# Alternating the half and the queue of the Toeplitz strip loads, and one eviction for two channels, in a long-convolution kernel

## The chip, the cores and the metric

The kernel runs on one core of a Trainium2 chip. The metric is the device time in microseconds (us) of the whole program. Executions of one kernel agree within about 0.3%, so effects below one per cent were timed in several rounds against the kernel before on the same chip. The record marks each timed run as fast or slow by its time and its granted clock. The stage lengths below are each read from one profiled execution; the experiment e4, which loads its strips as the kernel before does, has a stage 3 us longer, so differences of that size mean nothing.

## The reference, cut to what matters

```python
def _attn_ref(x, h):                  # x: (8, 5696, 128), h: (5696, 128), float32
    L = 2 * S                         # a causal convolution along the sequence, per channel d
    y = irfft(rfft(x, n=L, axis=1) * rfft(h, n=L, axis=0)[None], n=L, axis=1)[:, :S, :]
    return y
def _moe_ref(x, w_theta, w_tok_r, w_tok_i, w_ch):     # fed with the y of above
    theta = x @ w_theta
    y = einsum('ts,bsd->btd', w_tok_r, x*cos(theta)) + einsum('ts,bsd->btd', w_tok_i, x*sin(theta))
    u = x + y
    return u + maximum(u @ w_ch, 0)
```

The change touches only the first half, the convolution. The kernel computes it per channel `d` as a block-Toeplitz matrix product on the matmul engine.

## The kernel before: the parts that matter

Each channel needs 45 blocks of 128 x 128 weights. They are cut from "strips": partition `p` of a strip holds the padded filter `h_pad[d]` from position `j0 + p` on, so each partition holds the one above it shifted by one element. A strip serves 15 matmuls. Only 64 partitions are loaded from memory; the other 64 are the same data 64 columns later, and VectorE (DVE) copies them.

```python
    KS = 15                                                # blocks per strip, 3 strips per channel
    ...
    with tc.tile_pool(name="conv_sbuf", bufs=6) as csb, \
         tc.tile_pool(name="conv_psum", bufs=2, space=PSUM) as cps:
        for d in range(D):                                 # 128 channels
            psum = cps.tile([P, NT * B], F32, tag="convps")          # 128 x 360
            for k0 in range(0, NT, KS):
                k1 = k0 + KS; w = KS * P; j0 = P * k0
                strip = csb.tile([P, KS * P + 64], BF16, tag="strip")
                own, other, c0, c1 = (lower half, upper half, 0, 64) if d % 2 == 0 else \
                                     (upper half, lower half, 64, 0)
                nc.sync.dma_start(strip[own, :w + 64], bass.AP(...h_pad, d * HW + j0,     # L151
                                          ap=[[1, 64], [1, w + 64]]))   # 64 rows, 1 element apart
                nc.vector.tensor_copy(strip[other, c0:c0 + w], strip[own, c1:c1 + w])     # L154
                for k in range(k0, k1):
                    ntj = NT - k; c = c0 + (k - k0) * P
                    nc.tensor.matmul(psum[:, B * k: B * k + B * ntj], strip[:, c:c + P],  # L158
                                     x_sb2[:, d, :B * ntj],
                                     start=(k == 0), stop=(k == NT - 1))
            nc.scalar.activation(                                                         # L162
                y_sb[:, :, :, d].rearrange("q t b -> q (t b)"), psum, AF.Copy)
```

(The slices are spelled in words.) The moving operand shrinks from 360 columns at the first block to 8 at the last, so the first strip of a channel keeps the matmul engine much longer than the third. `y_sb` has the channel as its innermost dimension: the eviction of one channel (the copy of its finished sums out of `psum`) writes 360 single bf16 values per partition, 256 bytes apart.

## Time and profile before

| | before |
|---|---|
| time, median of its first 3 runs | 2369.0 us |
| convolution, first to last L158 matmul | 108.2 to 598.0 us, 490 us |
| the same without stalls (128 channels of 3.63 us) | 465 us |
| strip: bytes, median time from issue to landing | 254 KB, 4.6 us |
| one eviction (ScalarE, ACT) | 1.777 us |

The groups of the page (line, engine, operation, output<-input, shapes, count; busy us and mean ns of one; idle time of the engine just before them and what ended it) show the three lines that matter. PE is the matmul engine, DVE is VectorE, ACT is ScalarE:

```profile
L158 PE MATMUL psum<-x_sb,strip 128*128 128x360 bf16 (+44 forms) x5760 | 474.1, 243 | 17.0 <-DVE strip L154 15.2
...
L154 DVE COPY strip<-strip 64x1920 bf16<-64x1920 bf16 x384 | 250.7, 655 | 239.3 <-DMA strip<-h_pad 205.1
...
L162 ACT ACTIVATE y_sb<-psum 128x360 bf16<-128x360 f32 x128 | 227.4, 1777 | 264.4 <-PE psum L158 264.4
```

The eviction costs 1.777 us for 360 elements per partition. DVE waits 205 us for strip DMAs, but what counts is how much of that reaches PE. The view of the matmuls' line (duration min/median/max, first and last start) and the view by stretches (busy us and instruction count per engine, then granted clock, DMA share, GB/s) give the stage:

```profile
L158 PE MATMUL psum<-x_sb,strip x5760: 166/243/501, 108.2 to 598.0; 128*128 128x360 bf16 x5, 128*128 128x128 bf16 x5, 128*128 128x256 bf16 x5, 128*128 128x24 bf16 x5
```

```profile
core 0: us, PE busy (x) PEld busy (x) DVE busy (x) ACT busy (x) POOL busy (x), PEclk, DMA share, GB/s
108.00:598.00 490.00, 473.93 (x5760) 406.32 (x5759) 249.38 (x382) 225.78 (x128) 0.00 (x0) 0.99 0.75 199
```

PE is busy 474 of 490 us at a granted clock of 0.99 (the share of full speed that PE was given), so it bounds the stage. The timeline gives the pace that PE has when nothing disturbs it: four evictions in a row, each released by the last matmul of its channel, start 3.63 us apart (columns: start, duration, engine, line, operation, count, idle before and releaser):

```profile
117.96 1.78 ACT L162 ACTIVATE y_sb<-psum 128x360 bf16<-128x360 f32 x1 [1.73 <-PE psum L158]
...
121.59 1.78 ACT L162 ACTIVATE y_sb<-psum 128x360 bf16<-128x360 f32 x1 [1.85 <-PE psum L158]
...
125.22 1.77 ACT L162 ACTIVATE y_sb<-psum 128x360 bf16<-128x360 f32 x1 [1.85 <-PE psum L158]
...
128.84 1.78 ACT L162 ACTIVATE y_sb<-psum 128x360 bf16<-128x360 f32 x1 [1.86 <-PE psum L158]
```

128 channels at that pace are 465 us, so about 25 us of the stage are lost. The list of waits names what PE waits for (total us, times, longest):

```profile
engine line waited for: us in total, times, longest us
PE psum L158 <- DVE strip L154: 15.2, 33, 0.9
```

It is the copied strip, and behind the copy the strip's DMA. The timeline shows one such place: the copy starts only at 162.24 us, after 1.65 us of waiting for its DMA, and the next channel's first matmul follows 0.06 us after the copy's end:

```profile
162.24 0.65 DVE L154 COPY strip<-strip 64x1920 bf16<-64x1920 bf16 x1 [1.65 <-DMA strip<-h_pad]
...
162.95 1.30 PE L158 MATMUL psum<-x_sb,strip 128*128 128x360 bf16 x8 [0.55 <-DVE strip L154]
```

One strip of 254 KB per 1.21 us (a third of 3.63) is 210 GB/s; the stage moves 199 GB/s. The page's list of DMA issues (size, median us from issue to landing; its KB are 1024 bytes, so 248.0 KB are the 254 KB of the text):

```profile
strip<-h_pad SPq DMA_DIRECT2D x384, 248.0 KB, 4.6
```

### The profile page before, as it was taken

The page shows a single profiled execution, that of the slowest core. Times are in us where ns is not written, and L with a number is a line of the kernel's source. Part 1 is how long each engine was busy: PE and PEld are TensorE (multiplying, and loading weights), DVE is VectorE, ACT ScalarE, POOL GpSimd, SP SyncE. Part 2 cuts the span into 40 slices and gives each one's busy share as a digit, 9 for nine tenths or more (in the row PEclk, how much of TensorE's full clock was granted, in tenths as well). Part 3 has the DMA queues.
Part 4 walks back from the last instruction along what each step waited for, and adds up shares of the span by engine and source line. Part 5 has one row for each costly group of instructions (what it writes and reads, how often), then busy time and mean ns, then how long its engine had stood idle before and what let it go on. Part 6 is the DMA issues. An engine that isn't in the chain of part 4 may idle for free.

```text
span 2367.9 us, 39718 instructions
## 1 busy us (share of the span) xinstructions
PE 2191.0 (93%) x14513; PEld 1216.4 (51%) x14686; DVE 1649.6 (70%) x2997; ACT 639.2 (27%) x733; POOL 796.1 (34%) x1474
## 2 busy tenths in 40 slices
PE   4699999999666999999999999799999999999997
PEld 1188888888432444444444444234444444444443
DVE  5655555555577888887787776687677677677774
ACT  3544444444862333332232000001111111111111
POOL 0000000000201544544446564344544544544540
PEclk7599999999978999999999999899999999999998
DMA  9977777777998988988789997967877977977872
GB/s 238 251 204 203 200 204 202 202 197 202 232 284 218 164 156 168 164 165 156 134 168 164 159 151 128 286 101 134 156 136 130 160 134 134 160 132 136 151 135 54
DMA packets 435332, 405.51 MB, mean 171 GB/s; under 512 B 66497, under 2 KB 370625, under 8 KB 435009
## 3 DMA queue, kind: packets, MB, share of 16 engines
q0 software_dynamic: 222816, 131.33, 42.4%
q1 hardware_dynamic: 209296, 260.55, 38.9%
q10 hardware_dynamic: 3024, 11.08, 1.3%
q8 instruction: 116, 1.90, 0.3%
q14 instruction: 80, 0.65, 0.1%
HBM read 449.27 MB, written 84.75 MB: 226 GB/s over the span
## 4 chain that ended last, share of the span: by engine, by line
PE 70%; DMA 15%; DVE 8%; issue 3%; POOL 2%; ACT 1%; SPq 1%; DVEq 0%; ACTq 0%; POOLq 0%
PE m L598 51%; PE psum L158 14%; DMA strip<-h_pad 6%; DMA tmp<-in_x_dram 2%; DVE c L605 2%; POOL wb L326 2%; DMA wb<-in_moe_w_tok_r_dram 2%; DMA wb<-in_moe_w_tok_i_dram 2%; DMA h_bf<-in_h_dram 1%; DVE wt L335 1%; DVE strip L154 1%; PE v L419 1%; PE utp L412 1%; PE m L560 1%; PE m L562 1%
## 5 line engine op out<-in xcount | busy, mean ns | idle before, releaser
L326 POOL DMA_DIRECT2D wb<-in_moe_w_tok_i_dram x720 | 388.7, 547 | 801.7 <-DVE wt L335 713.8
L326 POOL DMA_DIRECT2D wb<-in_moe_w_tok_r_dram x720 | 387.6, 546 | 714.4 <-PE psum L158 594.3
L158 PE MATMUL psum<-x_sb,strip 128*128 128x360 bf16 (+44 forms) x5760 | 474.1, 243 | 17.0 <-DVE strip L154 15.2
L598 PE MATMUL m<-b,wt 128*128 128x512 bf16 x1892 | 453.7, 383 | 26.9 <-DVE wt L335 9.8
L158 PEld LDWEIGHTS <-strip 128*128 128x128 bf16 x5760 | 406.5, 98 | 85.4 <-DVE strip L154 21.2
L335 DVE STREAM_TRANSPOSE wt<-wb 128x384 f32<-128x384 f32 (+2 forms) x720 | 359.8, 524 | 123.1 <-PE m L598 73.5
L154 DVE COPY strip<-strip 64x1920 bf16<-64x1920 bf16 x384 | 250.7, 655 | 239.3 <-DMA strip<-h_pad 205.1
L598 PEld LDWEIGHTS <-wt 128*128 128x128 bf16 x1936 | 190.6, 99 | 259.8 <-issue 27.6
L162 ACT ACTIVATE y_sb<-psum 128x360 bf16<-128x360 f32 x128 | 227.4, 1777 | 264.4 <-PE psum L158 264.4
L605 DVE TENSOR_TENSOR c<-c,m 128x512 f32<-128x512 f32 x440 | 284.0, 671 | 0.0
L414 ACT ACTIVATE uts<-utp 128x512 bf16<-128x512 bf16 (+1 forms) x90 | 53.3, 592 | 616.7 <-PE utp L412 616.7
L409 ACT ACTIVATE ub<-c 128x512 bf16<-128x512 f32 (+1 forms) x90 | 56.5, 628 | 226.6 <-DVE c L605 226.3
L121 PE MATMUL rps<-tmpbf,R_bf 128*128 128x512 bf16 x88 | 45.7, 620 | 52.1 <-DVE tmpbf L118 52.0
L185 ACT ACTIVATE yT<-tpz 128x512 bf16<-128x512 bf16 x68 | 39.7, 596 | 191.5 <-PE tpz L181 191.5
L118 DVE CAST tmpbf<-tmp 128x1024 bf16<-128x1024 f32 x45 | 56.7, 1267 | 33.3 <-DMA tmp<-in_x_dram 33.1
L199 ACT ACTIVATE red<-theta_ps,magic 128x512 f32<-128x512 f32 x46 | 31.6, 687 | 151.3 <-PE theta_ps L197 116.9
L421 DVE SCALAR_TENSOR_TENSOR c<-v,c 128x512 f32<-128x512 f32 (+1 forms) x90 | 61.6, 684 | 11.3 <-PE v L419 10.8
L123 ACT ACTIVATE x_sb<-rps 128x1024 bf16<-128x1024 f32 x45 | 46.1, 1024 | 57.8 <-PE rps L121 50.1
L219 ACT ACTIVATE mag<-mag,half_pi 128x512 f32<-128x512 f32 (+1 forms) x68 | 57.8, 850 | 0.2
L605 DVE TENSOR_TENSOR c<-yy,m 128x512 f32<-128x512 bf16 x88 | 56.1, 679 | 0.9 <-PE m L598 0.9
L121 PEld LDWEIGHTS <-R_bf 128*128 128x128 bf16 x90 | 6.2, 111 | 89.5 <-DVE tmpbf L118 80.8
L217 ACT ACTIVATE mag<-red 128x512 f32<-128x512 f32 x46 | 29.0, 630 | 77.6 <-DVE red L201 77.6
(2759 smaller groups left out, 2967.7 us busy)
## 6 DMA issues: line engine op xcount, KB each, us to landing
strip<-h_pad SPq DMA_DIRECT2D x384, 248.0 KB, 4.6
wb<-in_moe_w_tok_r_dram POOLq DMA_DIRECT2D x352, 96.0 KB, 4.4
wb<-in_moe_w_tok_i_dram POOLq DMA_DIRECT2D x352, 96.0 KB, 4.6
wb<-in_moe_w_tok_r_dram POOLq DMA_DIRECT2D x352, 80.0 KB, 4.3
wb<-in_moe_w_tok_i_dram POOLq DMA_DIRECT2D x352, 80.0 KB, 3.7
tmp<-in_x_dram SPq DMA_DIRECT2D x44, 512.0 KB, 5.8
cp_hbm<-c SPq DMA_DIRECT2D x88, 256.0 KB, 2.5
c<-cp_hbm SPq DMA_DIRECT2D x88, 256.0 KB, 4.6
```

Of the source, the lines that this page charges most:

```text
L118: nc.vector.tensor_copy(tmpbf, tmp.transpose([0, 2, 1]))
L154: nc.vector.tensor_copy(strip[other, c0:c0 + w], strip[own, c1:c1 + w])
L158: nc.tensor.matmul(psum[:, B * k: B * k + B * ntj], strip[:, c:c + P], x_sb2[:, d, :B * ntj], start=(k == 0), stop=(k == NT - 1))
L162: nc.scalar.activation(y_sb[:, :, :, d].rearrange("q t b -> q (t b)"), psum, AF.Copy)
L219: nc.scalar.activation(mag, mag, AF.Sin, bias=half_pi, scale=-TWO_PI)
L326: nc.gpsimd.dma_start(wb[32 * i:32 * i + 32, :ng, :nj * 64], bass.AP(tensor=a.tensor, offset=a.offset + row0 * S + p * H + i * QR + j0 * 6 ...
L335: nc.vector.transpose(wt.rearrange("p j t r -> p (j t r)").bitcast(F32).rearrange("p (j g t) -> p g j t", j=TJ, g=4)[:, :ng, :nj], wb[:, : ...
L409: nc.scalar.activation(ub[:m].rearrange("p b d -> p (b d)"), c[:m], AF.Copy)
L414: nc.scalar.activation(uts[:, :, :m], utp[:, :, :m], AF.Copy)
L421: nc.vector.scalar_tensor_tensor(c[:m], v[:m], 0.0, c[:m], op0=ALU.max, op1=ALU.add)
L598: nc.tensor.matmul(ms[q], a[q][:, j, :, r], bts[jj][q][:, r, :], start=(jj == 0 and r == 0), stop=(jj == NJ - 1 and r == 1 and q not in left))
L605: nc.vector.tensor_tensor(c, z, ms[q], op=op)
```

## The change

The intent: let two strips in flight go to different halves of the partitions, so that the DMA engines can write both halves at once, and let two queues feed them; and halve the work of ACT by evicting two channels in one instruction, which then writes two neighbouring bf16 values (4 bytes) at each place.

```diff
         for d in range(D):
-            psum = cps.tile([P, NT * B], F32, tag="convps")
+            if d % 2 == 0:
+                pair = cps.tile([P, 2, 512], F32, tag="convps")
+            psum = pair[:, d % 2, :NT * B]
             for k0 in range(0, NT, KS):
 ...
-                own, other, c0, c1 = ((slice(0, 64), slice(64, P), 0, 64) if d % 2 == 0 else
+                n_ = d * 3 + k0 // KS
+                own, other, c0, c1 = ((slice(0, 64), slice(64, P), 0, 64) if n_ % 2 == 0 else
                                       (slice(64, P), slice(0, 64), 64, 0))
-                nc.sync.dma_start(strip[own, :w + 64],
+                eng = nc.sync if n_ % 2 == 0 else nc.scalar
+                eng.dma_start(strip[own, :w + 64],
 ...
-            nc.scalar.activation(
-                y_sb[:, :, :, d].rearrange("q t b -> q (t b)"), psum, AF.Copy)
+            if d % 2 == 1:
+                nc.scalar.activation(
+                    y_sb[:, :, :, d - 1:d + 1].rearrange("q t b e -> q (t b) e"),
+                    pair[:, :, :NT * B].rearrange("q e n -> q n e"), AF.Copy)
```

More of the change, by code (lines that the diff above doesn't have):

```diff
@@ L147 @@
                 strip = csb.tile([P, KS * P + 64], BF16, tag="strip")
-                own, other, c0, c1 = ((slice(0, 64), slice(64, P), 0, 64) if d % 2 == 0 else
+                n_ = d * 3 + k0 // KS
+                own, other, c0, c1 = ((slice(0, 64), slice(64, P), 0, 64) if n_ % 2 == 0 else
                                       (slice(64, P), slice(0, 64), 64, 0))
-                nc.sync.dma_start(strip[own, :w + 64],
-                                  bass.AP(tensor=h_pad.tensor, offset=h_pad.offset + d * HW + j0,
-                                          ap=[[1, 64], [1, w + 64]]))
+                eng = nc.sync if n_ % 2 == 0 else nc.scalar
+                eng.dma_start(strip[own, :w + 64],
+                              bass.AP(tensor=h_pad.tensor, offset=h_pad.offset + d * HW + j0,
+                                      ap=[[1, 64], [1, w + 64]]))
                 nc.vector.tensor_copy(strip[other, c0:c0 + w], strip[own, c1:c1 + w])
```

## The prediction

> **What bounds the kernel now.** The change touches only the convolution stage, from the first L158 matmul at 108.2 us to the last at 598.0 us (the view of line L158): 490 us of 2368. There the view by stretches gives PE 57.5 to 58.4 us busy in each 60 us at a granted clock of 1.00, ACT about 28. PE bounds the stage. In the timeline, undisturbed channels follow each other every 3.63 us (L162 starts at 117.96, 121.59, 125.22, 128.84), so 128 channels would take 465 us. Some 25 us of the stage are stalls; that is all the change can win, 1.1%.
>
> The stalls come from strips that arrive late: the list of waits has PE behind the L154 copy 33 times (15.2 us) and its weight loads 40 times (20.6 us); that copy waited 205 us for strip DMAs. A strip is 64 partitions x 3968 B = 254 KB. One every 1.21 us (the PE pace) is 210 GB/s; the stage runs at 200 to 204, with a median of 4.6 us from issue to landing, 3.3 us at best. The Trainium skill ("SBUF — State Buffer", "Door 1: The DMA port swizzle") says 64 partitions reach 8 of 16 ports, about 218 GB/s. The trace agrees: the transfers sit just under that. Three strips in a row use one half.
>
> **What changes.** Bytes, copies (655 ns) and matmuls stay. Halves alternate on every strip and two queues feed them, so two strips in flight can use different ports. The same page ("Can I just issue two DMAs to hit both halves?") measured only +6% for this. Even +6% on 200 GB/s is 212, just above what PE needs; I expect somewhat more, and landing about 3.5 to 4 us.
>
> ACT gets 192 issues (0.44 us each on SP now, about 85 us) and 64 double evictions for 128 of 1.777 us. One eviction of 360 elements into 2-byte pieces 256 B apart costs 4.4 ns an element, while L123 with 16-byte pieces costs 1.0; the cost is in the scattered write. Pairs have the same number of pieces, so my estimate is 1.8 to 2.1 us for a pair, saving about 100 us of ACT, all off the critical path.
>
> **The risk.** ACT works in order. The strip that reuses the buffer of a pair's last strip becomes issuable as the pair's eviction does, and probably queues behind it. Its loop is eviction + landing + copy 0.65 + its matmuls 0.6 + about 0.15: with 1.9 and 3.6 us that is 6.9 us, inside the 7.26 us that PE needs for a pair. If the pair's eviction took 3.4 us (every element paying the scattered price), the loop would be 8.3 us or more and add 65 us or more over 64 pairs.
>
> The end of the stage gains a double eviction and four PSUM banks instead of two held until then: under 1 us. Later stages should shift unchanged.
>
> **Predicted.** Most of the 25 us of stall goes, 5 to 7 us remain: 2350 us, 8 in 10 between 2338 and 2385. Faster by over 2% (under 2322) would need more than the stage's stalls: 0.03. Within 2%: 0.86. Slower: 0.11.
>
> **What would show it.** Right: first to last L158 matmul in about 470 us; PE's wait for L154 from 15 us to under 5; stage rate near 210 GB/s; median landing under 4.2 us; L162 x64 at about 1.9 us. Wrong: landing still 4.6 us and the same stalls (halves do not overlap: about 2369); or regular PE waits once per pair for a strip issued by ACT right after L162 (queue order); or L162 above 3 us.
>
> **What would make it wrong.** A slow pair eviction; late issues in ACT's in-order queue; engines that serialise the halves; a lower granted clock when PE has no gaps.

## The result, and the profile after

The median went from 2367.65 us (4 runs) to 2355.34 us (4 runs, 2354.32 to 2358.01). The ratio is 0.9943, with a 95% interval of 0.9928 to 0.9958: faster, though by less than 2%. Here and below a ratio is the mean time of one kernel's fast runs over that of the other's fast runs of the same rounds, so it is not quite the ratio of the medians. The kernel is 13.5 us faster (0.0057 of 2368), inside the predicted range of 2338 to 2385, but 5 us short of the predicted 2350.

The groups after, with the line numbers of the new kernel (L158 is now the copy, L162 the matmul, L167 the eviction):

```profile
L162 PE MATMUL pair<-x_sb,strip 128*128 128x360 bf16 (+44 forms) x5760 | 472.0, 243 | 8.9 <-DVE strip L158 7.0
...
L158 DVE COPY strip<-strip 64x1920 bf16<-64x1920 bf16 x384 | 251.5, 655 | 228.1 <-DMA strip<-h_pad 194.8
...
L167 ACT ACTIVATE y_sb<-pair 128x720 bf16<-128x720 f32 x64 | 50.9, 795 | 429.8 <-PE pair L162 368.1
```

The stage by the line of its matmuls and by stretches:

```profile
L162 PE MATMUL pair<-x_sb,strip x5760: 166/243/497, 108.1 to 587.7; 128*128 128x360 bf16 x5, 128*128 128x128 bf16 x5, 128*128 128x256 bf16 x5, 128*128 128x24 bf16 x5
```

```profile
core 0: us, PE busy (x) PEld busy (x) DVE busy (x) ACT busy (x) POOL busy (x), PEclk, DMA share, GB/s
108.00:588.00 480.00, 472.00 (x5760) 403.93 (x5759) 250.80 (x383) 50.25 (x65) 0.00 (x0) 1.00 0.72 203
```

PE's waits, and the DMA issues:

```profile
PE pair L162 <- DVE strip L158: 7.0, 18, 1.3
```

```profile
strip<-h_pad SPq DMA_DIRECT2D x192, 248.0 KB, 4.3
strip<-h_pad ACTq DMA_DIRECT2D x192, 248.0 KB, 4.3
```

The convolution went from 490 to 480 us. PE's wait for the copied strip halved, from 15.2 to 7.0 us, but did not go away. The landing time fell only from 4.6 to 4.3 us. The eviction, now of twice the data, takes 0.795 us, less than half of what one channel took before. So four questions are open. Which of the three parts made the gain? Why are about 15 us of stalls left (480 against 465)? Why is the pair eviction so cheap? And did the in-order ACT queue, the risk of the prediction, cost anything?

### The profile page after: what moved, and what is told of

Same layout as the page of the kernel before. It is cut to its first block, busy times and chain, and to the rows that moved or that the text cites. A ratio compares the mean times of both kernels' runs of the same rounds, so it can differ in the third digit from the quotient of the medians.

```text
span 2352.5 us, 39824 instructions
## 1 busy us (share of the span) xinstructions
PE 2191.6 (93%) x14686; PEld 1210.8 (51%) x14686; DVE 1650.1 (70%) x2997; ACT 462.6 (20%) x669; POOL 798.2 (34%) x1474
## 4 chain that ended last, share of the span: by engine, by line
PE 77%; DMA 13%; DVE 6%; issue 2%; ACT 1%; SPq 1%; POOL 1%; DVEq 0%; ACTq 0%; POOLq 0%
PE m L604 56%; PE pair L162 15%; DMA strip<-h_pad 4%; DMA tmp<-in_x_dram 2%; DMA wb<-in_moe_w_tok_r_dram 2%; DVE c L611 1%; DMA b<-zi_hbm 1%; DMA h_bf<-in_h_dram 1%; PE v L425 1%; PE utp L418 1%; PE m L566 1%; PE m L568 1%; PE m L608 1%; DMA wb<-in_moe_w_tok_i_dram 1%; DVE wt L341 1%
## 5 line engine op out<-in xcount | busy, mean ns | idle before, releaser
L162 PE MATMUL pair<-x_sb,strip 128*128 128x360 bf16 (+44 forms) x5760 | 472.0, 243 | 8.9 <-DVE strip L158 7.0
L162 PEld LDWEIGHTS <-strip 128*128 128x128 bf16 x5760 | 404.0, 98 | 77.6 <-DVE strip L158 12.9
L158 DVE COPY strip<-strip 64x1920 bf16<-64x1920 bf16 x384 | 251.5, 655 | 228.1 <-DMA strip<-h_pad 194.8
L167 ACT ACTIVATE y_sb<-pair 128x720 bf16<-128x720 f32 x64 | 50.9, 795 | 429.8 <-PE pair L162 368.1
L123 ACT ACTIVATE x_sb<-rps 128x1024 bf16<-128x1024 f32 x45 | 46.1, 1024 | 57.5 <-PE rps L121 57.2
```

## The experiments

Theories for the gain: **A**, two halves are written at once; **B**, the second queue; **C**, the shorter eviction. Each of the first four kernels has one part of the change, or all but one.

### e1: only the halves alternate

```diff
-   ... 0, 64) if d % 2 == 0 else
+   ... 0, 64) if (d * 3 + k0 // KS) % 2 == 0 else
```

> Edit: halves change with every strip, one queue (SP), one eviction per channel as before. Theory A (the gain is two halves written at once): about 2359 us, first to last matmul of the convolution from 490 us to about 481, PE's waits for the strip copy from 15 to about 7 us. Theory B (the gain is the second queue): no change, 2367 us. Theory C (the gain is the shorter eviction): no change.

Measured: 2355.78 us median (5 runs), ratio 0.9944, interval 0.9932 to 0.9956: the gain of the full change, with one queue and the old evictions. The matmuls' line and PE's waits:

```profile
L158 PE MATMUL psum<-x_sb,strip x5760: 166/243/497, 107.4 to 585.7; 128*128 128x360 bf16 x5, 128*128 128x128 bf16 x5, 128*128 128x256 bf16 x5, 128*128 128x24 bf16 x5
```

```profile
PE psum L158 <- DVE strip L154: 6.6, 19, 0.6
```

The stage is 478 us long and the waits are 6.6 us. Theory A holds as far as it says that the halves make the gain; they alone suffice.

### e2: only the queues alternate

```diff
-   nc.sync.dma_start(strip[own, :w + 64],
+   (nc.sync if (d * 3 + k0 // KS) % 2 == 0 else nc.scalar).dma_start(strip[own, :w + 64],
```

> Edit: strips in turn on two queues (SP, ACT), halves change per channel and one eviction per channel as before. Theory A: no gain, 2365 to 2370 us, perhaps a loss of a few us as ACT issues strips behind 1.78 us evictions. Theory B: about 2359 us, convolution about 481 us. Theory C: no change.

Measured: 2371.46 us median (6 runs), ratio 1.0009, interval 0.9997 to 1.0022. There is no gain, and PE's waits are, if anything, more:

```profile
PE psum L158 <- DVE strip L154: 19.6, 40, 1.0
```

(The window of this answer ends at 598 us; over the whole stage, which ends at 604.7 us, it is 20.4 us in 41 waits.) Theory B falls.

### e3: halves and queues, with the old evictions

The edit is the sum of the two above.

> Edit: both halves and queues alternate, one eviction per channel as before (1.78 us each). Theory A and B: the convolution gains about 10 us as in the full change (480 us), total about 2357 to 2360 us. If the strips that ACT issues behind a 1.78 us eviction come too late: PE waits per channel stay, total nearer 2367 us. Theory C: no gain.

Measured: 2360.15 us median (6 runs, 2358.49 to 2369.47), ratio 0.9972, interval 0.9956 to 0.9987. The stage takes 479 us in the profiled run (107.2 to 586.4), as with the halves alone; the six runs scatter more than those of any other kernel of this job. The second queue with the long evictions is not better than the halves alone, and its time is some 4 to 7 us longer (medians 2360.15 and 2355.78 us, means 2362.4 and 2355.8), though the two intervals touch. Why is not settled. It is not the eviction that holds back ACT's issues, as the prediction feared. The timeline shows an eviction and the next issue of ACT's queue (ACTq):

```profile
302.50 1.79 ACT L162 ACTIVATE y_sb<-psum 128x360 bf16<-128x360 f32 x1 [1.84 <-PE psum L158]
302.56 0.45 ACTq L151 DMA_DIRECT2D strip<-h_pad  x1
```

The issue starts 0.06 us after the eviction *starts*, while the 1.79 us eviction is still running. In the full change it is the same:

```profile
304.22 0.79 ACT L167 ACTIVATE y_sb<-pair 128x720 bf16<-128x720 f32 x1 [7.14 <-PE pair L162]
304.28 6.08 ACTq L155 DMA_DIRECT2D strip<-h_pad  x3
```

Counted in the packed trace of the full change, 63 of the 64 evictions are followed by an issue of ACT's queue within 0.1 us of their start (after the last one there is nothing to load). So the queue passes from the eviction to the DMA issue as soon as the eviction has started. The eviction's duration is not in the loop.

### e4: only the pair eviction

The edit is the first and the last hunk of the change.

> Edit: strips as before, only the eviction is shared by two channels (about 0.80 us for 720 elements). Theory A and B: the convolution stays at 490 us; only its end is 1.0 us shorter (one eviction of 0.8 in place of 1.8 us on the way to the next stage), total about 2366 us. Theory C: the convolution goes to about 480 us, total about 2356 us.

Measured: 2368.15 us median (5 runs), ratio 0.9993, interval 0.9980 to 1.0006: no difference that the rounds can tell from none. The stage did not get shorter: it took 493 us in the profiled run (108.5 to 601.7), which was the slowest of the five, and the eviction is the fast one of the full change:

```profile
L165 ACT ACTIVATE y_sb<-pair 128x720 bf16<-128x720 f32 x64 | 50.9, 795 | 443.4 <-PE pair L160 443.4
```

Theory C falls: the 177 us that ACT saves (227.4 to 50.9) are off the critical path.

### p1 to p4: the transfers by themselves

To measure the disputed cost alone, four probes keep all 384 strip loads but do only one matmul of 15 per strip and copy only the 128 columns that it needs. Their outputs are wrong, which doesn't matter for the times. All use the pair eviction; they differ only in the halves and queues. ("The page" in the last expectation is the one that the prediction cites for +6%.)

```diff
-   nc.vector.tensor_copy(strip[other, c0:c0 + w], strip[own, c1:c1 + w])
-   for k in range(k0, k1):
+   nc.vector.tensor_copy(strip[other, c0:c0 + P], strip[own, c1:c1 + P])
+   for k in range(k0, k0 + 1):
```

> Probe of the transfers alone, wrong result on purpose: one matmul of 15 and a 128-column copy per strip, pair eviction, strips as before (half by channel, one queue). 384 strips of 254 KB. If one half at a time limits: about 1.2 us a strip, 210 to 218 GB/s, stage about 460 us. If it is the buffers times latency (6 buffers, 4.6 us) the stage would be clearly shorter.

> The probe with halves changing per strip, one queue. Theory A: clearly above the rate of the probe with the old strips, 240 GB/s or more (stage under 410 us). If one queue serialises the halves: the same 210 GB/s.

> The probe with two queues and the half by channel. Theory A: as the probe with the old strips, about 210 GB/s. Theory B: faster.

> The probe with both. Theory A with packets of the two queues interleaved: the fastest of the four, 240 GB/s or more; if the page's 6% holds, 220 to 225 GB/s.

The same stretch of the stage in each probe, by the view by stretches (the columns are those shown above; the last three are granted clock, DMA share and GB/s). As before (p1):

```profile
210.00:450.00 240.00, 77.72 (x204) 21.22 (x204) 38.50 (x204) 26.23 (x34) 0.00 (x0) 0.50 1.02 216
```

Halves alternate, one queue (p2):

```profile
210.00:450.00 240.00, 85.37 (x224) 23.21 (x223) 42.23 (x224) 28.59 (x37) 0.00 (x0) 0.50 1.02 237
```

Two queues only (p3):

```profile
210.00:450.00 240.00, 77.72 (x204) 21.24 (x204) 38.74 (x205) 26.25 (x34) 0.00 (x0) 0.50 1.03 217
```

Both (p4):

```profile
210.00:450.00 240.00, 86.30 (x227) 23.50 (x226) 42.80 (x226) 28.79 (x38) 0.00 (x0) 0.50 1.02 240
```

With the matmuls and most of the copying out of the way the old pattern moves 216 GB/s, just above the 210 that PE needs. Alternating halves moves 237 on one queue, which is 10% more; the second queue alone moves 217, which is nothing; both move 240, which is 11% more. This agrees with e1 and e2: the halves make the gain. That the two halves lie behind different ports is not seen in any trace; the rates only agree with it. My expectation for p2 was "240 GB/s or more (stage under 410 us)"; it was missed by 3 GB/s (the stage, first to last matmul, took 411 us). The stage of p1 took 449 us.

### p5: does the source hold the two halves to 240 GB/s?

Two halves could have given more than 10%. One suspect is the source: 64 rows that start 2 bytes apart. The probe reads 64 rows that start 256 bytes apart instead (again a wrong result).

```diff
-   offset=h_pad.offset + d * HW + j0,         ap=[[1, 64], [1, w + 64]]
+   offset=h_pad.offset + (d % 120) * HW + j0, ap=[[P, 64], [1, w + 64]]
```

> The transfer probe with both halves and both queues (240 GB/s), but its 64 rows start 256 bytes apart in h_pad instead of 2 bytes. If what holds the two halves to 240 GB/s is the source (rows that start at odd places and overlap): 280 GB/s or more, stage from 405 us to under 350. If it is on the receiving side or in the engines: the same 240 GB/s.

```profile
210.00:450.00 240.00, 84.22 (x222) 22.98 (x221) 41.89 (x221) 28.59 (x37) 0.00 (x0) 0.50 1.02 235
```

235 GB/s: not faster. The odd starts of the rows are not what holds the rate. That the rows overlap is not excluded: 3968-byte rows that start 256 bytes apart still do. In all five probes six strips are in flight or in use (there are six buffers), and the DMA share is 1.02 or 1.03; whether more strips in flight would raise the rate was not tried, since a seventh buffer does not fit in memory (the pool asks for 27.125 KB per partition and 27 are left).

### f1: halves and pair eviction on one queue

```diff
-   eng = nc.sync if n_ % 2 == 0 else nc.scalar
+   eng = nc.sync
```

> Edit: the full change with all strips on one queue (SP): halves alternate, pair eviction. If the second queue adds nothing: as the full change or the halves alone, 2354 to 2356 us. If ACT's issues cost something that the short eviction gave back: a little faster than both, 2352 to 2354 us. If the second queue is needed with pair evictions: 2358 us or more.

Measured: 2350.61 us median (5 runs), ratio 0.9929, interval 0.9917 to 0.9940. Taking the second queue out of the change does not cost anything; it is perhaps 3 us better, but its interval overlaps that of the full change (0.9928 to 0.9958). The profiled stage is the shortest so far, 473 us, and its waits are 2.8 us:

```profile
L162 PE MATMUL pair<-x_sb,strip x5760: 166/243/498, 107.4 to 580.5; 128*128 128x360 bf16 x5, 128*128 128x128 bf16 x5, 128*128 128x256 bf16 x5, 128*128 128x24 bf16 x5
```

```profile
PE pair L162 <- DVE strip L158: 2.8, 9, 0.5
```

In all three pairs that differ by the second queue alone (e2 and the kernel before, e3 and e1, the full change and f1) the kernel with two queues is the slower one by its ratio: 1.0009 against 1, 0.9972 against 0.9944, 0.9943 against 0.9929. No single pair shows it clear of its intervals.

### f2: the same with smaller strips

Some 13 us of stalls were left in e1, 15 in the full change and 8 in f1 (478, 480 and 473 us against 465). f2 changes f1, and f1 is what it has to be compared with. Two theories: **R1**, a buffer is tied up until the last of its 15 matmuls, so the next load into it starts too late; **R2**, what is left is transfer rate. Strips of 9 blocks with 10 buffers take nearly the same memory (24,320 against 23,808 bytes per partition), and 2% more bytes are moved. That would hurt under R2 and help under R1.

```diff
-   KS = 15
+   KS = 9
-   conv_sbuf bufs=6
+   conv_sbuf bufs=10
-   n_ = d * 3 + k0 // KS
+   n_ = d * (NT // KS) + k0 // KS
```

> Edit: the previous run with strips of 9 blocks instead of 15 and 10 buffers instead of 6 (the same memory within 3%, 2% more bytes). About 12 us of stall are left in the convolution. Theory R1 (a buffer is tied up until the last of its 15 matmuls, so the loads start too late): stalls shrink by half or more, first to last matmul about 472 us, total about 2348 us. Theory R2 (what is left is transfer rate): no gain or a loss, 2355 us or more.

Measured: 2340.06 us median (4 runs, 2339.24 to 2343.59), ratio 0.9882, interval 0.9869 to 0.9894. This beats f1, timed in the same rounds, by about 11 us (0.9929 less 0.9882, times 2368; the intervals lie apart). It beats the kernel before by 28 us (0.0118 of 2368), and the changed one by about 14 (0.9943 less 0.9882, times 2368; these two ran in different jobs, each against the kernel before). The chain of waits (start, duration, what) now holds the whole convolution as one piece:

```profile
108.34 465.98 PE pair L162 x5760
```

All 5760 matmuls follow each other in 466 us without a wait for a strip. That is the 465 us that the undisturbed pace of before promised. The stage and the DMA issues:

```profile
108.00:574.00 466.00, 465.66 (x5754) 403.50 (x5754) 289.39 (x637) 50.42 (x64) 0.00 (x0) 1.00 0.67 213
```

```profile
strip<-h_pad SPq DMA_DIRECT2D x640, 152.0 KB, 3.5
```

The rate rose to 213 GB/s, all that PE takes at this pace with 2% more bytes, so the transfers could give more all along (237 GB/s in p2); a strip lands after 3.5 us. R1 explains it and R2 falls. R1 needs one reservation. Smaller strips free buffers sooner, but they also land sooner (3.5 against 4.1 us in f1) and are copied faster (455 against 655 ns). All three shorten the way from a free buffer to a usable strip, and this run does not tell them apart.

### f3: still smaller strips, on two queues

Strips of 5 blocks, 17 buffers, and the two queues of the change, as 1152 issues of 0.44 us would fill one queue.

> Edit: the full change (two queues, since 1152 issues of 0.44 us would fill one) with strips of 5 blocks and 17 buffers (same memory, 6.5% more bytes, rows of 1.4 KB). R1: total 2345 to 2350 us. R2 or a loss of rate through short rows: 2360 us or more, landing rate under 225 GB/s.

Measured: 2397.57 us median (6 runs), ratio 1.0119, interval 1.0098 to 1.0140: slower, with a stage of 522 us (107.9 to 629.5). The R1 expectation failed and the other one came true: the view by stretches has 196 to 208 GB/s in every 60 us from 160 us on. It is a loss of its own, not the R2 that f2 had refuted. The waits of SP's queue from 100 to 600 us (total us, times, longest) show something that is rare elsewhere:

```profile
SPq L155 <- PE pair L162: 160.8, 378, 2.1
SPq L155 <- DMA strip<-h_pad: 118.6, 220, 2.6
```

SP waited 220 times for the landing of a strip before it could issue another one. The same view over the whole span shows one such wait in the full change (3.5 us) and none in f2.

The packed trace settles what these waits are. It holds, for each load, the semaphore that counts its landing (a semaphore is a counter through which one queue or engine tells another that work is done) and the semaphores that are waited for before it. In this program each queue uses four of them in turn when two queues load strips, and the one queue uses eight when it loads them alone. In f3 the queue waits, before all but one of the 1152 loads, for the semaphore that the load is about to use, so for the landing of the load four places earlier in the same queue. Of the 1144 loads that have one, none was issued before that landing and 757 came less than 0.2 us after it. Elsewhere this cost nothing: the landing lay at least 4.6 us back in the full change and 0.5 us in f2.

So the program let at most eight strips be in flight. Eight strips of 90,112 bytes that land after 3.3 us make 218 GB/s, by estimate, and PE would need 223 (1152 strips in 466 us). Two thirds of the loads went out as soon as that landing let them, so it was mostly this limit, and not want of buffers, that held them back: from the end of a buffer's last matmul to the issue of the next load into it the median is 2.3 us in f3, 0.14 in f2 and 0.04 in the full change. f3 therefore did not test whether smaller strips help under R1, and it does not show that short rows cost rate. 5 blocks on one queue, or with more semaphores, were not tried.

## Why the prediction was right or wrong

**Right: where the time is and how much there is to win.** The prediction put the ceiling at 25 us, from the 3.63 us pace against 490 us. f2 reached that ceiling: 466 us. The measured gain of 13.5 us is inside the range, and the sign and the class ("within 2%") were right.

**Right in kind: the halves.** The prediction expected a gain because "two strips in flight can use different ports". e1 and p2 show the gain from the halves; the ports themselves no trace shows. The Trainium skill ("SBUF — State Buffer", "Door 1: The DMA port swizzle") gives about 218 GB/s for 64 partitions; p1 measured 216. For two concurrent transfers on two halves the same page gives 6% over a single one ("Can I just issue two DMAs to hit both halves?"); p2, with a stream of strips, measured 10% and p4 11%.

**Mis-sized: "Most of the 25 us of stall goes, 5 to 7 us remain".** About 15 us remained: the stage took 480 us, not "about 470", and PE's wait was 7.0 us, not "under 5". The step that failed is the use of a mean rate. I took a rate above 210 GB/s as enough. With strips of 15 blocks the stalls persist though the rate is available (237 GB/s in p2), and f2 shows that they vanish with strips of 9. The term of the sum that was mis-sized is the landing time: "about 3.5 to 4 us", measured 4.3. Without the second queue most of the prediction's signs come true: f1 has a stage of 473 us, a wait of 2.8 us, a median landing of 4.1 us and 2350.6 us in all. So a part of the miss may be the second queue's cost, which the prediction counted as help; f1 and the full change were timed in different jobs and their intervals overlap, so this is not shown.

**Wrong: the price of the pair eviction.** The prediction wrote "the cost is in the scattered write. Pairs have the same number of pieces, so my estimate is 1.8 to 2.1 us". Measured: 0.795 us. There are 360 pieces 256 bytes apart in both cases, so the number of pieces alone cannot be the cost. (The prediction's 4.4 ns leaves out the start of the instruction. L185 and L123, which write 512 and 1024 elements in pieces of 16 bytes or more, take 596 and 1024 ns, which leaves some 170 ns for it by estimate; 1777 less 170, over 360, is 4.5 ns.) The skill would have told me: "SBUF — State Buffer", "Specifications (TRN2)", says that memory lines are 16 bytes long and at least two hits per line are needed for full bandwidth. One bf16 per line is one hit, a pair is two. The trace agrees: 1.777 us for 360 elements against 0.795 us for 720. The second figure is near the full rate of the skill, by an estimate from its figures: it ("ScalarE: Activation LUTs", "What ACT_TABLE_LOAD costs") gives 186 ns + 0.833 ns per element for an instruction with immediate scale and bias, which for 720 elements is 786 ns. The runs do not tell a line that is hit twice from a 4-byte word that is filled; both fit. The saving lies off the critical path, so the mistake cost the prediction nothing.

**Wrong: the risk.** "ACT works in order ... Its loop is eviction + landing + copy". The trace of e3 shows an issue that starts 0.06 us into an eviction of 1.79 us, so the eviction does not belong in that sum. With evictions of 1.78 us the stage was still 479 us long. The one chance in nine that I gave to a loss of over 2% through this loop rested on a mechanism that is not there.

**Not seen: the second queue brings nothing.** The prediction let "two queues feed them" stand as part of the gain. e1, e2, p3 and f1 show that the queue can be left out, and f1 that the kernel is then perhaps faster. The skill says so ("DMA: Bandwidth & Descriptors", "Issuing engines are not separate DMA queues"): issuing on several engines saves only issue time. p3 against p1 (217 and 216 GB/s) agrees.

**Nearly right: the later stages.** From the last matmul of the convolution to the end of the span are 1769.9 us before and 1764.8 after. Without the pair eviction this rest is 1768.3 to 1771.4 us in the profiled runs of before, e1, e2 and e3. With it (after, e4, f1, f2) it is 1763.4 to 1768.6; the two ranges just overlap. About 1 us is visible at once: the next stage's first transpose starts 2.0 us after the last matmul before (598.0 to 599.99) and 1.0 us after it in the new kernel (587.75 to 588.76), since the last eviction is 1 us shorter. The timed runs do not confirm more than that (e4: interval 0.9980 to 1.0006).

## What to carry to other kernels

When a stage sits a few per cent under the rate that it needs from loads of 64 partitions, try first to change the partition half from one load to the next: it costs one expression, and here a second queue added nothing to it. When stalls remain although the mean rate is enough, look at how long a buffer is tied up between its load and its last reader; more and smaller buffers in the same memory took the last stalls away here. When smaller loads make it worse, look in the trace at what an issue waits for: in f3 it was mostly the program's own few semaphores, so that run says little about the size. And when an eviction writes single 2-byte values far apart, write two neighbours at once: here twice the data took less than half of the time, which is worth something wherever ACT is on the critical path (here it is not).

## What the Trainium skill lacked or had wrong

- "SBUF — State Buffer", "Can I just issue two DMAs to hit both halves?" and "DMA: Bandwidth & Descriptors", "Rules for kernel authors" advise against transfers to disjoint halves (the first with +6% for two concurrent transfers, the second with "Don't bother — they serialize"). In a steady stream of 254 KB strips, alternating halves moved 237 GB/s on one queue and 240 on two, against 216 on one half per channel (10% and 11%), and the kernel gained 0.56% (e1).
- "SBUF — State Buffer", "Specifications (TRN2)" gives the rule of two hits per 16-byte line, and I found no price for a ScalarE write on any page. Here a ScalarE eviction that writes one bf16 every 256 bytes took 1.777 us for 360 elements, and one that writes pairs took 0.795 us for 720.
